# Sums of the second pass's right-hand blocks: made beside the output layer and kept in DRAM, or made beside the first down layer

## The chip, the cores and the metric

The kernel runs on one core of one Trainium2 chip. The metric is the time of one execution in microseconds, as the device measures it. All products run on TensorE in single precision (fp32r operands, fp32 sums in PSUM).

## The reference

`q`, `k`, `v` have 4 batches, 12 heads, 448 positions and 64 channels; the token matrix `x` has 1792 rows (4 batches of 448) and 768 columns.

```python
attn = sigmoid(q @ k.T / 8 - log(448)) @ v          # per batch and head, then heads side by side: x
xn   = x / sqrt(mean(x*x) + 1e-6) * rms_g
g    = xn @ w_gate                                  # 768 -> 1536
y    = (g * sigmoid(g) * (xn @ w_val)) @ w_out      # 1536 -> 768
a, b = y @ w1, y @ w2                               # 768 -> 1024
out  = (a * b @ w3) @ moe2_w_out                    # 1024 -> 1024 -> 768
```

The kernel multiplies `w3` by the second `w_out` once and keeps the product in DRAM, so that the last two layers are one layer of 1024 to 768.

## The kernel before, in words

**Tiles.** Activations lie transposed: 128 channels by the 448 tokens of one batch (0.22 MB in fp32). Each operand of an exact product is a pair of fp32r tiles, a high part (a copy on ScalarE) and a low part (the block less its high part: on VectorE for activations, on GpSimd for most weights), and each product of two 128-wide blocks is three matmuls of 448 columns: high by high, low by high, high by low (`runs`, L340, whose matmul is L346).

**Passes.** Batches 0 and 1 are the first pass (g = 0), batches 2 and 3 the second (g = 1). Where a layer is worked by Strassen-Winograd, the two batches of the pass are the two columns of blocks, and seven products stand for eight. The output layer of the first block is not: its second pass, `b_units(1)`, is twelve groups of 36 matmuls (`b_group`, L810), `j` 0 to 11, with m = j // 2 the block of 128 output channels and b = j % 2 the batch. A group's result goes from PSUM to a scratch tile on ScalarE (`yf`, L815) and by a DMA of SyncE's queue to DRAM (`yd`, L817).

**The layers after it**, in program order: eight `c_winograd` for the first pass (`a` and `b` of `y`, the up layers), three `d_winograd(0)` (the first down layer, which writes the first half of the output), eight `c_winograd` for the second pass and three `d_winograd(1)`. In the up layers a product is 9 matmuls (L689 calls `runs`), in the down layers 6; each Winograd step has seven products, and a `d_winograd` runs them twice, the second time adding to the same seven PSUM banks. `combine` (L716) takes the seven results from PSUM: one by ScalarE (`u`, L722) and the rest by VectorE (`v` L725, `c` L729, `u` L732, `c` L735, `u` L739, `v` L740 and L744). A bank is free for the next product when the instruction that reads it is done.

**Right-hand blocks.** An up layer needs for each k of 0 to 2 seven right-hand tiles, from the four blocks of `y` that belong to k (m = k and k + 3, both batches): the four blocks themselves and four sums of them. Each of the seven becomes a high part (ScalarE, L584) and a low part (VectorE, L576): 21 such pairs. For the first pass this is `y_blocks(0, k)` (L655), which runs beside the output layer of the second pass, after j = 2, 5 and 8. For the second pass it is `y_steps(k)` (L668), spread over the first down layer by `step` (L661): `combine` and `d_winograd` call `step` once per product, and each call runs the first generator of the list `todo` up to its next `yield`. Before that list reaches `y_steps`, it ends `right_steps` for the down layer's own operands.

**Buffers and order.** `held` (L92) is a tag of four buffers of one block each; the blocks of `y` come through it, and so do three of every four products `a * b` in the up layers (`ab`, L764). `scratch` (L89) is a tag of six. The Tile framework decides each engine's order by a planner, which takes instructions as its model sees them ready, in the order of the program where several are; an instruction may thus come long before its place in the program. `tc.keep_in_program_order` ties an instruction behind the one traced before it on its engine; the subtractions of `y_steps` are tied so. Each engine, and SyncE's queue with nearly all DMAs, then works its list strictly in order.

Of the kernel before, what the change touches and what calls it, by code (L numbers as in the profile page):

```python
# [9 lines left out]
F32 = mybir.dt.float32  # L10
F32R = mybir.dt.float32r
U32 = mybir.dt.uint32
AF = mybir.ActivationFunctionType
ALU = mybir.AluOpType
PSUM = bass.MemoryType.PSUM

B, H, S, D = 4, 12, 448, 64
P = 128
# [27 lines left out]
def fused_kernel(ctx: ExitStack, tc: tile.TileContext, qkv, wg, wv, wo, w1, w2, w3, wo2, gam, out):  # L46
    nc = tc.nc
# [15 lines left out]
    dram = tc.alloc_tile_pool(name="dram", bufs=1, space=bass.MemoryType.DRAM)  # L63
# [21 lines left out]
    def parts(pool, tag, bufs, name, w=S, step=0):  # L85

        return pool.tile([P, 2, w + step], F32R, tag=tag, bufs=bufs, name=name)[:, :, :w]

    def scratch(name):  # L89
        return scr.tile([P, S], F32, tag="s", bufs=6, name=name)  # L90

    def held(name):  # L92
        return scr.tile([P, S], F32, tag="held", bufs=4, name=name)
# [438 lines left out]
    acts = {}  # L532

    def x_tile(name, b):
        return parts(r1a, "x0", 6, name, step=STEP) if b == 0 else parts(r1b, "x1", 6, name)
# [24 lines left out]
    def right_tile(name, bl):  # L560
        p, n, step = {0: (r1a, 6, STEP), 1: (r1b, 6, 0), 2: (pools["xw"], 9, STEP)}[bl]
        return parts(p, f"x{bl}", n, name, step=step)

    def ab_tile(name, n):

        if n < 2 * KF1:
            return h_tile(name, n // 2)
        return right_tile(name, (n - 2 * KF1) // 2)

    def right_steps(k, b, home=None, down=False, wait=None):  # L570

        def sub(out, in0, in1, op=ALU.subtract):
            i = nc.vector.tensor_tensor(out=out, in0=in0, in1=in1, op=op)  # L576
            if down or wait is not None:
                tc.keep_in_program_order(i)

        late = []  # L580

        def put(j, bl, src):
            t = acts["d" if down else "w", j, k] = ab_tile(f"w{j}", 7 * k + j) if down else right_tile(f"w{j}", bl)
            nc.scalar.activation(t[:, 0, :], src, AF.Copy)  # L584
            low()
            late.append((t, src))

        def low():
            if late:
                t, src = late.pop()  # L590
                sub(t[:, 1, :], src, t[:, 0, :])

        if wait is None:
            put(0, 0, b[0])
            yield
            t1 = home()
            sub(t1, b[1], b[0])
            put(5, 1, t1)
            yield
            while len(b) < 4:  # L600
                low()
                yield
            put(2, 0, b[2])
            yield
            t3 = home()
            sub(t3, b[3], b[1])
            put(3, 2, t3)
            yield
            t2 = home()
            sub(t2, t3, b[0], ALU.add)  # L610
            put(1, 2, t2)
            yield
            t4 = home()
            sub(t4, b[2], t2)
            put(4, 2, t4)
            yield
            put(6, 1, b[3])
            yield
            low()
            return  # L620
        t1 = scratch("t1")
        sub(t1, b[1], b[0])
        t2 = scratch("t2")
        sub(t2, b[3], t1)
        put(1, 2, t2)
        yield
        sub(b[1], b[3], b[1])
        put(3, 2, b[1])
        yield
        sub(t2, b[2], t2)  # L630
        put(4, 2, t2)
        yield
        for _ in range(wait):
            low()
            yield
        for j, bl, x in ((0, 0, b[0]), (2, 0, b[2]), (5, 1, t1), (6, 1, b[3])):
            put(j, bl, x)
            yield
        low()

    def x_blocks(k):
        for _ in right_steps(k, [load_x(b, m) for m in (k, k + 3) for b in (2, 3)], bank):
            pass

    yd = {}

    def load_y(g, k):
        y = []
        for m in (k, k + 3):
            for b in range(2):  # L650
                y.append(held("ys"))
                nc.sync.dma_start(out=y[-1], in_=yd.pop((g, b, m)))
        return y

    def y_blocks(g, k):  # L655
        for _ in right_steps(k, load_y(g, k), bank):
            pass
# [3 lines left out]
    def step():  # L661

        if todo:
            next(todo[0], None)
            if inspect.getgeneratorstate(todo[0]) == inspect.GEN_CLOSED:
                todo.pop(0)

    def y_steps(k):  # L668
        y = load_y(1, k)
        for _ in range(2):  # L670
            yield
        yield from right_steps(k, y, wait=5 if k == 2 else 0)

    def product_bank():
        return psm()[:, :S]
# [149 lines left out]
    def b_units(g):  # L825
        for m in range(KD):
            for b in range(2):
                yield 6.8, (lambda m=m, b=b: b_group(g, m, b)), (i_b2 if g else i_b)[m][1]

    def run(unit, more=0):  # L830
        cost, fn, wi = unit
        W.load_to(wi + 2 + more)
        fn()
        W.split_to(wi + 1 + more)
        W.load_to(wi + 3 + more)
        return cost
# [50 lines left out]
    for k in range(KD):  # L887
        t = acts["x", 1, k] = x_tile("x", 1)
# [24 lines left out]
    b = list(b_units(0))  # L913
# [35 lines left out]
    for j, u in enumerate(b_units(1)):  # L949
        run(u, 1)  # L950
        if j in (2, 5, 8):
            y_blocks(0, j // 3)


    for m in range(KF2):
        c_winograd(i_c, m)
    todo.extend(y_steps(k) for k in range(KD // 2))
    for n in range(KD // 2):
        d_winograd(0, i_d, n)
# [64 lines left out]
```

## Time and profile before

| | |
|---|---|
| median of 3 runs | 1059.55 us (1058.46 to 1061.62) |
| the profiled execution | 1058.72 us, of which the span from the first to the last instruction is 1056.9 us |
| busy, share of the span | PE 99%, PEld 84%, DVE 77%, ACT 42%, POOL 38% |
| output layer, second pass | 654.1 to 742.3 us |
| up layers, first pass | 742.3 to 845.1 us |
| first down layer | 845.1 to 899.1 us |

How to read it: PE is TensorE's matmul row and PEld its weight loads, DVE is VectorE, ACT ScalarE, POOL GpSimd and SP SyncE, which issues the DMAs. PE's busy time includes modelled ends of pipelined matmuls, so it can hide small waits; the number of matmuls in a stretch, or the busy time of PEld, shows them. A wait is listed with the engine that waits and, behind the arrow, what released it.

### The profile page before, as it was taken

The numbers are of one execution on the slowest core, as the hardware profiler recorded it, in microseconds if no ns is written. First come the engines' busy times: TensorE is split into PE (matmuls) and PEld (weight loads), VectorE is DVE, ScalarE is ACT, GpSimd is POOL, SyncE is SP. The second block draws the span as 40 slices with busy tenths as digits, with TensorE's granted clock in tenths as the row PEclk, the third lists the DMA queues.
The fourth block names the chain that finished last, engine by engine and source line by source line (L and its number), as shares of the span: only waits on it lengthen the run. The fifth ranks groups of instructions, "written<-read, shape, count | busy, mean of one in ns | idle before, by whom it ended". The sixth has DMA issues, their size and how long they took to land. (4 is left out here: it accounts for less than half of the span.)

```text
span 1056.9 us, 14300 instructions
## 1 busy us (share of the span) xinstructions
PE 1047.1 (99%) x5150; PEld 890.0 (84%) x5150; DVE 813.6 (77%) x1172; ACT 442.2 (42%) x800; POOL 398.9 (38%) x342
## 2 busy tenths in 40 slices
PE   9999999999999999999999999999999999999998
PEld 4338799998777777798999999999999998999997
DVE  5998988777665787788677778973688999677764
ACT  5684332223454553335444443332344455344431
POOL 2646400000222221102555554232555666555562
PEclk9999999999999999999999999999999999999999
DMA  7653555665454567763122113867333344533131
GB/s 262 243 185 106 180 185 182 209 225 206 146 164 147 182 216 253 251 231 111 65 65 71 69 68 105 273 230 245 129 120 120 94 132 144 164 108 115 52 95 70
DMA packets 72934, 164.26 MB, mean 155 GB/s; under 512 B 7200, under 2 KB 45216, under 8 KB 72864
## 3 DMA queue, kind: packets, MB, share of 16 engines
q1 hardware_dynamic: 70560, 160.20, 45.6%
q10 hardware_dynamic: 2304, 3.15, 0.8%
q8 instruction: 41, 0.67, 0.3%
q14 instruction: 29, 0.24, 0.1%
HBM read 119.67 MB, written 43.65 MB: 155 GB/s over the span
## 5 line engine op out<-in xcount | busy, mean ns | idle before, releaser
L346 PE MATMUL w<-w,ws 128*128 128x448 f32 x2052 | 420.6, 366 | 1.6 <-DVE v L725 1.6
L346 PEld LDWEIGHTS w<-w,ws 128*128 128x128 f32 x2052 | 385.0, 188 | 35.1 <-DVE v L725 2.0
L139 POOL TENSOR_TENSOR ws<-wd,ws 128x384 fp32r<-128x384 f32 (+1 forms) x160 | 154.7, 983 | 157.0 <-ACT ws L135 146.3
L346 PE MATMUL psm<-hm,ws 128*128 128x448 f32 x864 | 178.3, 367 | 0.5 <-DVE ws L139 0.5
L346 PEld LDWEIGHTS psm<-hm,ws 128*128 128x128 f32 x864 | 161.9, 188 | 16.7 <-issue 2.0
L346 PE MATMUL psm<-x,ws 128*128 128x448 f32 x648 | 136.3, 368 | 0.4 <-DVE s L794 0.4
L346 PEld LDWEIGHTS psm<-x,ws 128*128 128x128 f32 x648 | 120.9, 188 | 15.1 <-issue 2.9
L139 POOL TENSOR_TENSOR ws<-wf,ws 128x768 fp32r<-128x768 f32 (+1 forms) x51 | 94.7, 1860 | 98.5 <-ACT ws L135 97.5
L135 ACT ACTIVATE ws<-wf 128x768 fp32r<-128x768 f32 (+1 forms) x81 | 66.5, 825 | 99.5 <-PE psm L346 21.1
L135 ACT ACTIVATE ws<-wd 128x384 fp32r<-128x384 f32 (+1 forms) x160 | 71.0, 476 | 65.7 <-PE w L346 47.0
L428 POOL TENSOR_TENSOR qk<-qk 128x960 fp32r<-128x960 f32 x10 | 23.8, 2381 | 189.9 <-ACT qk L427 189.9
L115 DVE TENSOR_SCALAR mag<-wd 128x768 uint32<-128x768 uint32 (+1 forms) x76 | 47.1, 619 | 49.1 <-DMA wd<-in_wo 18.1
L139 POOL TENSOR_TENSOR ws<-s,ws 128x384 fp32r<-128x384 f32 (+1 forms) x64 | 63.4, 990 | 49.3 <-ACT ws L135 45.9
L125 DVE SCALAR_TENSOR_TENSOR wf<-wd,wf 128x768 uint32<-128x768 uint32 (+1 forms) x76 | 79.4, 1045 | 2.3
L117 DVE TENSOR_SCALAR wf<-mag 128x768 uint32<-128x768 uint32 (+1 forms) x76 | 62.6, 823 | 16.3 <-POOL ws L139 11.1
L128 DVE SCALAR_TENSOR_TENSOR wf<-wd,wf 128x768 uint32<-128x768 uint32 (+1 forms) x76 | 73.6, 969 | 1.1
L346 PEld LDWEIGHTS psm<-o,ws 128*128 128x128 f32 x384 | 67.3, 188 | 2.4 <-issue 2.3
L346 PE MATMUL psm<-o,ws 128*128 128x384 f32 x384 | 69.3, 339 | 0.0
L509 POOL TENSOR_TENSOR acc<-acc,sq 128x448 f32<-128x448 f32 x20 | 27.1, 1357 | 85.0 <-ACT sq L508 85.0
L180 DVE TENSOR_TENSOR wd<-wd,s 128x384 f32<-128x384 f32 (+1 forms) x32 | 26.8, 837 | 33.8 <-POOL ws L139 33.8
L116 DVE TENSOR_SCALAR mag<-mag 128x768 f32<-128x768 f32 (+1 forms) x76 | 50.6, 665 | 1.7
L462 ACT ACTIVATE a<-sc,bias_s 128x896 f32<-128x896 f32 x48 | 45.4, 997 | 8.4 <-PE sc L442 8.4
(122 smaller groups left out, 1278.1 us busy)
## 6 DMA issues: line engine op xcount, KB each, us to landing
wd<-in_wo SPq DMA_DIRECT2D x20, 768.0 KB, 5.4
wd<-in_w SPq DMA_DIRECT2D x16, 768.0 KB, 5.3
wd<-in_wg SPq DMA_DIRECT2D x12, 768.0 KB, 4.5
wd<-in_wv SPq DMA_DIRECT2D x12, 768.0 KB, 5.2
raw<-in_qkv SPq DMA_DIRECT2D x12, 736.0 KB, 4.3
wd<-in_w SPq DMA_DIRECT2D x16, 512.0 KB, 4.4
w<-wf SPq DMA_DIRECT2D x16, 384.0 KB, 2.6
wd<-w SPq DMA_DIRECT2D x16, 384.0 KB, 3.5
```

The costliest lines, as they stand in the source:

```text
L115: nc.vector.tensor_scalar(out=mag.bitcast(U32), in0=hi, scalar1=0x7FFFFFFF, scalar2=None, op0=ALU.bitwise_and)
L116: nc.vector.tensor_scalar(out=mag, in0=mag, scalar1=HI_MIN, scalar2=HI_MAX, op0=ALU.max, op1=ALU.min)
L117: nc.vector.tensor_scalar(out=u, in0=mag.bitcast(U32), scalar1=3, scalar2=0x3FFFFFFF, op0=ALU.logical_shift_left, op1=ALU.bitwise_and,)
L125: nc.vector.scalar_tensor_tensor(out=u, in0=hi, scalar=0xC0000000, in1=u, op0=ALU.bitwise_and, op1=ALU.bitwise_or)
L128: nc.vector.scalar_tensor_tensor(out=u, in0=lo, scalar=29, in1=u, op0=ALU.logical_shift_right, op1=ALU.bitwise_or)
L135: nc.scalar.activation(t[:, 0, :w], f[:, :w], AF.Copy)
L139: lows.tensor_tensor(out=t[:, 1, :w], in0=f[:, :w], in1=t[:, 0, :w], op=ALU.subtract)
L180: nc.vector.tensor_tensor(out=a12, in0=a12, in1=s2, op=ALU.subtract)
L346: nc.tensor.matmul(ps, w, xt[:, xi, :], start=first and r == 0 and j == 0, stop=last and r == 2 and j == n - 1)
L428: nc.gpsimd.tensor_tensor(out=lo, in0=x, in1=hi, op=ALU.subtract)
L462: nc.scalar.activation(a, both, **sigmoid)
L509: nc.gpsimd.tensor_tensor(out=acc[b], in0=acc[b], in1=sq, op=ALU.add)
```

## The change

`right_steps` loses its second form, in which the seven tiles came in another order with the sums made in place; it now serves the first pass and the down layers alone. A new function `y_sums(k)` loads the four blocks of the second pass for k, makes the four sums on VectorE and stores them in DRAM. It is called in the output layer after the groups j = 7 (k = 0) and j = 9 (k = 1), and after the last group (k = 2). `y_steps(k)` then loads seven blocks (three sums first, then the four others, the last sum among these) one by one, three ahead, and only copies and subtracts.

```diff
-    def right_steps(k, b, home=None, down=False, wait=None):
+    def right_steps(k, b, home, down=False):
...
-        t1 = scratch("t1")
-        sub(t1, b[1], b[0])
-        t2 = scratch("t2")
-        sub(t2, b[3], t1)
-        put(1, 2, t2)
-        yield
-        sub(b[1], b[3], b[1])
-        put(3, 2, b[1])
-        yield
-        sub(t2, b[2], t2)
-        put(4, 2, t2)
-        yield
-        for _ in range(wait):
-            low()
-            yield
-        for j, bl, x in ((0, 0, b[0]), (2, 0, b[2]), (5, 1, t1), (6, 1, b[3])):
-            put(j, bl, x)
-            yield
...
+    y_src = {}
+
+    def y_sums(k):
+
+        src = y_src[k] = {j: yd[1, b, m] for j, (b, m) in zip((0, 5, 2, 6), ((0, k), (1, k), (0, k + 3), (1, k + 3)))}
+        y = load_y(1, k)
+        t1, t2, t4 = (scratch(n) for n in ("t1", "t2", "t4"))
+        tt = nc.vector.tensor_tensor
+        tt(out=t1, in0=y[1], in1=y[0], op=ALU.subtract)
+        tt(out=t2, in0=y[3], in1=t1, op=ALU.subtract)
+        tt(out=y[1], in0=y[3], in1=y[1], op=ALU.subtract)
+        tt(out=t4, in0=y[2], in1=t2, op=ALU.subtract)
+        for j, t in ((1, t2), (3, y[1]), (4, t4), (5, t1)):
+            src[j] = dram.tile([P, S], F32, name=f"ysum{k}{j}")
+            nc.sync.dma_start(out=src[j], in_=t)
+
     def y_steps(k):
-        y = load_y(1, k)
+
+        late, order = [], ((1, 2), (3, 2), (4, 2), (0, 0), (2, 0), (5, 1), (6, 1))
+
+        def load(n):
+            t = held("ys")
+            nc.sync.dma_start(out=t, in_=y_src[k][order[n][0]])
+            return t
+
+        def low():
+            if late:
+                t, src = late.pop()
+                tc.keep_in_program_order(nc.vector.tensor_tensor(out=t[:, 1, :], in0=src, in1=t[:, 0, :], op=ALU.subtract))
+
+        blocks = [load(n) for n in range(3)]
         for _ in range(2):
             yield
-        yield from right_steps(k, y, wait=5 if k == 2 else 0)
+        for n, (j, bl) in enumerate(order):
+            for _ in range(5 if n == 3 and k == 2 else 0):
+                low()
+                yield
+            t = acts["w", j, k] = right_tile(f"w{j}", bl)
+            src = blocks.pop(0)
+            nc.scalar.activation(t[:, 0, :], src, AF.Copy)
+            low()
+            late.append((t, src))
+            if n + 3 < len(order):
+                blocks.append(load(n + 3))
+            yield
+        low()
...
         if j in (2, 5, 8):
             y_blocks(0, j // 3)
+        if j in (7, 9):
+            y_sums((j - 7) // 2)
+    y_sums(2)
```

## Rows read from the trace of the kernel before

**Rows 1.** The page's first part: busy us (share of the span) xinstructions.
```profile
PE 1047.1 (99%) x5150; PEld 890.0 (84%) x5150; DVE 813.6 (77%) x1172; ACT 442.2 (42%) x800; POOL 398.9 (38%) x342
```

**Rows 2.** Who waited for whom, PE alone, 654 to 900 us.
```profile
PE w L346 <- DVE v L725: 1.6, 1, 1.6
PE psm L346 <- DVE c L735: 0.2, 1, 0.2
```

**Rows 3.** Busy time by stretch: length, then PE, PEld, DVE, ACT, POOL; clock, DMA.
```profile
654.00:742.30 88.30, 88.30 (x435) 81.22 (x434) 62.11 (x89) 26.66 (x48) 27.07 (x16) 1.00 0.70 240
742.30:845.10 102.80, 102.80 (x505) 94.50 (x504) 85.80 (x136) 41.64 (x90) 59.62 (x59) 1.00 0.37 118
845.10:899.10 54.00, 52.19 (x254) 46.91 (x253) 51.60 (x80) 27.55 (x65) 35.66 (x36) 1.00 0.47 141
...
879.47:890.53 11.06, 9.25 (x43) 7.57 (x42) 10.59 (x20) 2.14 (x7) 7.18 (x8) 1.00 0.67 209
```

**Rows 4.** The chain that ended last: start, duration, engine, tile, line, instructions.
```profile
899.24 107.59 PE w L346 x528
```

**Rows 5.** PE in order of time in the first down layer: start, duration.
```profile
870.92 5.04 PE L346 MATMUL w<-w,ws 128*128 128x448 f32 x24
...
879.47 1.40 PE L346 MATMUL w<-w,ws 128*128 128x448 f32 x6
882.44 3.98 PE L346 MATMUL w<-w,ws 128*128 128x448 f32 x18 [1.57 <-DVE v L725]
```

**Rows 6.** VectorE in order of time, the same stretch.
```profile
871.03 1.16 DVE L576 TENSOR_TENSOR t<-ys 128x448 f32<-128x448 f32 x1
...
881.77 0.61 DVE L725 TENSOR_TENSOR v<-w,u 128x448 f32<-128x448 f32 x1
```

**Rows 7.** VectorE by shape, 845 to 899 us: busy us, mean ns, idle before.
```profile
L576 DVE TENSOR_TENSOR t<-ys,t 128x448 f32<-128x448 f32 x6 | 4.2, 701 | 0.5 <-DMA ys<-y 0.4
...
L576 DVE TENSOR_TENSOR ys<-ys 128x448 f32<-128x448 f32 x3 | 2.4, 798 | 0.0
L576 DVE TENSOR_TENSOR t<-ys 128x448 f32<-128x448 f32 x3 | 2.4, 797 | 0.0
```

**Rows 8.** Tile ys, 845 to 899 us: its queue instruction, issue to landing.
```profile
L652 SPq DMA_DIRECT2D ys<-y x11: 319/332/455, 850.1 to 886.1; - x11
DMA to landing us min/median/max: 2.4/2.9/4.6
```

**Rows 9.** Tile yf, 654 to 760 us: its store, issue to landing.
```profile
DMA to landing us min/median/max: 1.9/3.4/5.2
```

**Rows 10.** Who waited for whom, SyncE's queue, 844 to 899 us.
```profile
SPq L652 <- DVE t L576: 7.6, 3, 6.1
```

**Rows 11.** ScalarE in order of time, output layer.
```profile
713.08 0.53 ACT L815 ACTIVATE yf<-psm 128x448 f32<-128x448 f32 x1
719.65 0.85 ACT L135 ACTIVATE ws<-wf 128x768 fp32r<-128x768 f32 x1 [6.04 <-DMA wf<-wo]
```

**Rows 12.** SyncE's queue in order of time, output layer.
```profile
715.22 0.86 SPq L817 DMA_DIRECT2D y<-yf  x2
```

**Rows 13.** VectorE in order of time: y_blocks(0, 2), first and last of its eleven.
```profile
698.94 0.63 DVE L576 TENSOR_TENSOR w<-ys 128x448 f32<-128x448 f32 x1 [0.49 <-DMA ys<-y]
...
703.45 1.33 DVE L576 TENSOR_TENSOR w<-w,w 128x448 fp32r<-128x448 f32 x2
```

**Rows 14.** All engines in order of time around the start of the up layers.
```profile
742.46 0.54 ACT L815 ACTIVATE yf<-psm 128x448 f32<-128x448 f32 x1 [2.63 <-PE psm L346]
...
743.59 0.40 SPq L817 DMA_DIRECT2D y<-yf  x1
...
746.19 0.62 DVE L725 TENSOR_TENSOR v<-w,u 128x448 f32<-128x448 f32 x1 [3.06 <-PE w L346]
...
757.04 0.63 DVE L744 TENSOR_TENSOR psm<-w,v 128x448 f32<-128x448 f32 x1
758.04 0.62 DVE L764 TENSOR_TENSOR ab<-psm,u 128x448 f32<-128x448 f32 x1
```

More of the change, by code (lines that the diff above doesn't have):

```diff
@@ L568, in ab_tile @@
         return right_tile(name, (n - 2 * KF1) // 2)
-    def right_steps(k, b, home=None, down=False, wait=None):
+    def right_steps(k, b, home, down=False):
         def sub(out, in0, in1, op=ALU.subtract):
             i = nc.vector.tensor_tensor(out=out, in0=in0, in1=in1, op=op)
-            if down or wait is not None:
+            if down:
                 tc.keep_in_program_order(i)
@@ L591, in low @@
                 sub(t[:, 1, :], src, t[:, 0, :])
-        if wait is None:
-            put(0, 0, b[0])
-            yield
-            t1 = home()
-            sub(t1, b[1], b[0])
-            put(5, 1, t1)
-            yield
-            while len(b) < 4:
-                low()
-                yield
-            put(2, 0, b[2])
-            yield
-            t3 = home()
-            sub(t3, b[3], b[1])
-            put(3, 2, t3)
-            yield
-            t2 = home()
-            sub(t2, t3, b[0], ALU.add)
-            put(1, 2, t2)
-            yield
[L613 to L620, printed above, removed]
-        t1 = scratch("t1")
-        sub(t1, b[1], b[0])
-        t2 = scratch("t2")
-        sub(t2, b[3], t1)
+        put(0, 0, b[0])
+        yield
+        t1 = home()
+        sub(t1, b[1], b[0])
+        put(5, 1, t1)
+        yield
+        while len(b) < 4:
+            low()
+            yield
+        put(2, 0, b[2])
+        yield
+        t3 = home()
+        sub(t3, b[3], b[1])
+        put(3, 2, t3)
+        yield
+        t2 = home()
+        sub(t2, t3, b[0], ALU.add)
         put(1, 2, t2)
         yield
-        sub(b[1], b[3], b[1])
-        put(3, 2, b[1])
+        t4 = home()
+        sub(t4, b[2], t2)
+        put(4, 2, t4)
         yield
-        sub(t2, b[2], t2)
-        put(4, 2, t2)
+        put(6, 1, b[3])
         yield
-        for _ in range(wait):
-            low()
-            yield
-        for j, bl, x in ((0, 0, b[0]), (2, 0, b[2]), (5, 1, t1), (6, 1, b[3])):
-            put(j, bl, x)
-            yield
         low()
@@ L666, in step @@
                 todo.pop(0)
-    def y_steps(k):
-        y = load_y(1, k)
+    y_src = {}
[11 more added lines that the diff above has]
+            nc.sync.dma_start(out=src[j], in_=t)
+    def y_steps(k):
+        late, order = [], ((1, 2), (3, 2), (4, 2), (0, 0), (2, 0), (5, 1), (6, 1))
[8 more added lines that the diff above has]
+        blocks = [load(n) for n in range(3)]
         for _ in range(2):
             yield
-        yield from right_steps(k, y, wait=5 if k == 2 else 0)
+        for n, (j, bl) in enumerate(order):
+            for _ in range(5 if n == 3 and k == 2 else 0):
+                low()
+                yield
+            t = acts["w", j, k] = right_tile(f"w{j}", bl)
[5 more added lines that the diff above has]
+                blocks.append(load(n + 3))
+            yield
+        low()
     def product_bank():
```

## The prediction

> **What bounds the kernel now.** I read the page's first part, then the waits of PE, then the stretches, and last the order of time around the one stretch that stood out. PE is busy for 99% of the span [rows 1], so only time that PE loses can be won. From the output layer to the end of the first down layer PE's own waits are two, 1.6 us for VectorE's `v` (L725) and 0.2 us for `c` (L735), both in the first down layer [rows 2].
>
> The stretches show the same loss in another way. The undisturbed rate of matmuls is on the chain of waits: 528 in 107.59 us, 0.2038 us each [rows 4]. The first down layer is 3 steps x 2 x 7 products x 6 matmuls = 252 matmuls, which is 51.35 us at that rate; the stretch takes 54.00 [rows 3]. It loses 2.65 us, 2.50 of them in one window of 42 matmuls, which should be 8.56 us and is 11.06 [rows 3]. VectorE is busy there for 51.60 of 54.00 us (96%), against 70% in the output layer (62.11 of 88.30) and 83% in the up layers [rows 3]. So in the first down layer VectorE is the limit, and nowhere near the change does PE lose anything else.
>
> Here two readings differ. PE's busy time says 1.81 us is lost (54.00 less 52.19) [rows 3]; the weight loads say more: 94.50 of 102.80 us (91.9%) in the up layers, so 49.64 would be due in 54.00, and 46.91 are there, 2.73 us missing [rows 3]. The Trainium skill, Perfetto Trace Analysis, section Identifying the Most-Contended Engine, says that a matmul row's busy share is no good measure of headroom and the weight loads' share is. By its rule the most to be won is 2.7 us, by PE's busy time 1.8; the count of matmuls above agrees with the rule.
>
> **How the stall comes about.** In the fourth run of seven products (from 870.92 us) the second product ends at 870.92 + 12 x 0.204 = 873.4 us [rows 5]. VectorE takes it from its bank only at 881.77 [rows 6], 8.4 us later. The next step's second product wants that bank at 879.47 + 1.22 = 880.7 and starts at 882.44 [rows 5]: 1.75 us late. Ahead of `v` on VectorE stand the tied subtractions of `y_steps`, the sums for k = 1 from 871.03 on among them [rows 6].
>
> **What the change removes there.** Four sums for each k, twelve in all: 4.2 + 2.4 + 2.4 = 9.0 us, 0.75 each [rows 7]. VectorE's load falls to 42.6 of 54 us, 79%, below the 83% at which the up layers run without a wait of PE. Eight of the twelve (k = 0 and 1) stand before the late `v`: 6.0 us less ahead of it, where 1.75 would do. The wait goes, with 4.25 us to spare. Gain: 2.5 us, up to 2.65; the sum takes 2.4, as some of the small losses around it may not be VectorE's.
>
> **What it adds there.** 21 loads for 12, so nine more of 0.22 MB, 2 MB in 54 us on DMA engines at 47% [rows 3]: about 38 GB/s on 141. ScalarE's copies and the low parts are as many as before. New is that each low part hangs on its own load. The loads n = 4 to 6 of each k wait until the low part of block n - 4 is done, which is traced with the copy of block n - 3, three products (3.66 us) before the copy that wants the load. A load takes 0.33 us of issue and 2.9 us to land (2.4 to 4.6) [rows 8]: 3.23 us, inside by 0.4 at the median, late by 1.27 at the longest. The first load of a next k is traced two products (2.44 us) before its copy: late by 0.8 at the median and 2.5 at the longest, if the planner doesn't bring it forward; the two behind it have a product more each. A late load holds ScalarE's copy, and behind it the weights' high parts; then the tied low part, and behind it on VectorE `v`, `c` and `u`, which free PE's banks. Ahead of the `v` in question are three loads of the first kind (k = 0) and one of the second (k = 1). From both sides: nothing, or 3 x 1.27 + 2.5 = 6.3 us, more than the 4.25 spare. At the medians it is 0.8, which the spare covers, so I take nothing.
>
> SyncE's queue is in order, and the loads stand in it among the stores of the output and the loads of weights. Before the change a load of `ys` held that queue for up to 6.1 us while a buffer was in use [rows 10]. Now each load wants one buffer where four were wanted together; I cost this at nothing, and at one such hold, 6.1 us less the spare 4.25, about 1.9, on the other side.
>
> **What it adds in the output layer.** Twelve sums (7 to 9 us) on a VectorE with 26 us idle of 88; twelve loads and twelve stores on DMA engines at 70% [rows 3]. PE needs neither. Weights are far ahead: the high part split at 719.65 is for matmuls some 12 us later (the last of twelve halves, first used half way into the group j = 10; groups are 88.2 / 12 = 7.35 us, so at 742.3 - 11.0 = 731.3) [rows 11], so SyncE's queue may be held some microseconds. Cost nothing.
>
> The loads read what was just stored. For j = 7 ScalarE's copy is at 713.08 [rows 11] and its store issued at 715.22 [rows 12]; landing takes 3.4 us (1.9 to 5.2) [rows 9], and then the load its 3.2. So `y_sums(0)` has its last block at about 722. It comes before `y_blocks(0, 2)` in the program, and both want all four `held` buffers. If the planner gives them in that order, `y_blocks(0, 2)`, now at 698.94 to 704.8 on VectorE [rows 13], moves behind it: three sums to 724.5, a store to 728 (it frees y[1]), a load to 731.5, then 6 us of work as now: 737.5. The first up layer starts at 742.3 [rows 14]: 4.8 us to spare. Cost nothing.
>
> `y_sums(2)` falls into the first up layer: result copied at 742.46, stored from 743.59 [rows 14], landed 747, loaded 750.2, sums of 2.5 us on VectorE by 753. VectorE takes a product there 0.3 us after it is done (`v` at 746.19 for a product done at 742.26 + 3.67) [rows 14], and a bank is wanted again three products, 5.5 us, later. So 2.5 us of sums fit, and a blocked VectorE costs PE only beyond about 3 to 4.5 us: the seventh product, done at 755.1 and read until 757.67 [rows 14], is wanted back at about 760.5, 2.9 us on. Cost nothing; on the other side 3 us, if the last load is late by a landing more.
>
> **The sum.** Profiled execution 1058.72 us (span 1056.9 and 1.8 around it) less 2.4 is 1056.3. That execution is 0.8 us under the median of the runs, so on the median, 1059.55, I forecast 1057.1.
>
> **Rivals.**
> Loads take the place of the sums. If the new loads ahead of that `v` are late by more than the 4.25 us spare together (of 6.3 at the longest), the stall at 880.7 comes back for another reason. For: the median has only 0.4 us in hand, and a hold of SyncE's queue adds to it. Against: the planner may issue a load as soon as its buffer is free, and products without a copy between two k's let it catch up. Time: 1059.5, 1061 with one hold of the queue.
>
> The buffers' chain, the slower one. `held` goes from `y_sums(0)` to `y_blocks(0, 2)`, `y_sums(1)`, `y_sums(2)` and the first `ab` (second one at 758.04 [rows 14]), each time over a store and a load. It decides at 742.3 us: two holds of SyncE's queue of the longest kind shown, 6.1 us [rows 10], are 12.2 us against the 4.8 to spare, so PE would wait 7.4 us for the first up layer's operands. With the 2.4 won later: 1059.55 + 7.4 - 2.4 = 1064.5. For: five users of four buffers in 45 us, each behind a DMA. Against: VectorE and SyncE have much idle time there, and the planner knows of the buffers. The Trainium skill, DMA: Bandwidth & Descriptors, section Anatomy of one DMA — SWDGE (gpsimd) path, speaks for this rival: a DMA signals only once its last byte is confirmed in the target, slowest where that is HBM, so a block stored and read back pays that twice. By its fit (2.0 us and bytes over 436 GB/s) an estimate is 2.5 us a landing, 5 for both; the rows have 3.4 and 2.9 [rows 8, 9], so the trace is dearer still.
>
> The sums do not leave the busy stretch: the planner puts them late, with the stall unchanged: 1059.5. Against: in the output layer all their inputs but those of k = 2 are there over 100 us before use.
>
> **How the numbers follow.** Forecast 0.63; late loads 0.16; the buffers' chain 0.17; sums that stay 0.04. A measurement of this kernel tells about 0.3% from no change, 3.2 us. The most that can be won, 2.65, is under that; with the runs' spread of 3 us a quarter of the forecast's cases still measures as faster: 0.15. Slower by over 3.2 us is the buffers' chain from 5.6 us of waiting on, 0.12, and late loads that hold more than these bounds, 0.04: 0.16. Within: 0.69. The range: 1055.4 (2.65 won, and 1.5 for the spread of the runs) to 1062.0, which takes in late loads with one hold and leaves out most of the slow chain.
>
> **What would show it.** Right: no wait of PE for L725 in the first down layer; the stretch at 51.4 to 51.7 us for its 252 matmuls; VectorE near 79% there with idle time behind loads of `ys`; the output layer at 88 and the up layers at 102.8 us. Wrong: a PE gap at the start of the first up layer, or a low part waiting on `ys` ahead of a late `v`.

## The result, and the profile after

The changed kernel takes 1070.46 us (median of 5 runs, 1069.48 to 1073.44), the kernel before beside it 1059.82 (5 runs, 1058.46 to 1061.62): ratio 1.0106, 95% interval 1.0090 to 1.0121. The forecast was 1057.1 with a range to 1062.0. It is slower, by about 10.6 us, and the sign was wrong.

The profiled execution after took 1072.52 us, its span is 1070.6. Against the span before, 1056.9, the 13.7 us divide so, by four marks: the first matmul of the output layer, the first of the up layers, the first into a `psm` tile of the first down layer, and the last of that layer:

| stretch | before | after | difference |
|---|---|---|---|
| start to output layer | 654.08 | 656.13 | +2.05 |
| output layer | 88.18 | 88.18 | 0 |
| start of the up layers to the down layer's `psm` | 107.74 | 120.48 | +12.74 |
| first down layer | 49.08 | 47.91 | -1.17 |
| the rest | 157.8 | 157.9 | +0.1 |

The 2.05 us ahead of the output layer lie where the program is the same. Of the kernels below, some that are no slower start their up layers as late, at 744.97 and 743.80 against 742.26, so I take this as a spread between executions and not as the change's. The question is the 12.74.

The first view is the page's first part; it answers to [rows 1]: busy us, share of the span, instructions.
```profile
PE 1050.7 (98%) x5150; PEld 891.7 (83%) x5150; DVE 812.5 (76%) x1172; ACT 442.5 (41%) x800; POOL 393.0 (37%) x342
```
The counts are those of before: the change only moves instructions. VectorE is as busy as ever, so this line names no culprit. PE's waits from 656 to 930 us do, as in [rows 2]: engine and line, who released it, us in total, times, the longest.
```profile
PE w L346 <- DVE v L744: 6.7, 1, 6.7
PE w L346 <- ACT u L741: 2.4, 1, 2.4
PE w L346 <- DVE u L751: 0.6, 1, 0.6
PE psm L346 <- DVE c L754: 0.3, 1, 0.3
```
`v` (L744) is the `v` of L725 before, `u` (L741) that of L722. The name is the one that the forecast expected to vanish, but the place is another: in order of time PE shows both waits just after the start of the up layers, after 36 and 45 matmuls (four and five products) (start, duration; in brackets the idle time before, and its releaser).
```profile
744.31 7.50 PE L346 MATMUL w<-w,ws 128*128 128x448 f32 x36
754.20 3.14 PE L346 MATMUL w<-w,ws 128*128 128x448 f32 x9 [2.40 <-ACT u L741]
764.07 36.13 PE L346 MATMUL w<-w,ws 128*128 128x448 f32 x166 [6.72 <-DVE v L744]
```
The waits are 9.1 us of the 12.74. The rest stands in the stretches (length, then busy us and instructions of PE, PEld, DVE, ACT and POOL, granted clock, DMA share, GB/s), which answer to [rows 3]:
```profile
764.07:769.68 5.61, 5.61 (x18) 5.04 (x18) 3.65 (x7) 1.51 (x3) 1.19 (x2) 0.60 0.38 124
...
864.79:912.70 47.91, 47.10 (x230) 42.59 (x228) 38.37 (x62) 26.12 (x60) 29.86 (x33) 1.00 0.66 198
```
After the waits TensorE runs at a granted clock of 0.60: 18 matmuls in 5.61 us, where 18 x 0.2038 = 3.67 are due [rows 4], 1.9 lost. The nine of 754.20 took 3.14 us for 1.83, 1.3 lost. 9.1 + 1.9 + 1.3 = 12.3 of 12.74. The last line is the first down layer: PEld 42.59 of 47.91 us (88.9%) against 86.9% before [rows 3], whose stretch begins 24 matmuls earlier, and VectorE is 80% busy.

Who holds `v`? VectorE in order of time, from just before the wait to its end:
```profile
753.06 0.61 DVE L654 TENSOR_TENSOR t<-ys 128x448 f32<-128x448 f32 x1
755.53 1.34 DVE L180 TENSOR_TENSOR wd<-wd,s 128x384 f32<-128x384 f32 x1 [1.86 <-POOL ws L139]
761.78 0.63 DVE L655 TENSOR_TENSOR t<-ys,t 128x448 f32<-128x448 f32 x1 [4.90 <-DMA ys<-y]
...
763.39 0.62 DVE L744 TENSOR_TENSOR v<-w,u 128x448 f32<-128x448 f32 x1
```
L654 to L657 are the sums of `y_sums(2)`. They stand ahead of `v` in VectorE's list, and the second of them waits for the last block of `y`, which reached SBUF at 761.8. SyncE's queue in order of time shows why so late:
```profile
749.16 0.32 SPq L660 DMA_DIRECT2D ysum<-t  x1
749.60 0.37 SPq L836 DMA_DIRECT2D y<-yf  x1
...
753.17 0.40 SPq L177 DMA_DIRECT2D sums<-wd  x1
...
754.49 0.69 SPq L836 DMA_DIRECT2D y<-yf  x1
...
759.33 0.32 SPq L630 DMA_DIRECT2D ys<-y  x1
```
The last block is stored at 754.49 and asked for again at 759.33. ScalarE had its copy ready at 747.12 + 0.53 = 747.65, by its own order of time:
```profile
747.12 0.53 ACT L834 ACTIVATE yf<-psm 128x448 f32<-128x448 f32 x1
...
752.79 0.52 ACT L135 ACTIVATE ws<-s 128x384 fp32r<-128x384 f32 x1 [4.31 <-DVE s L173]
...
753.63 0.52 ACT L741 ACTIVATE u<-w 128x448 f32<-128x448 f32 x1
```
So the store is 6.8 us late, and in the queue it comes behind `sums<-wd` (L177), whose operand VectorE made only after the sums of `y_sums(1)`; the store before it, of block j = 10, stands right behind the last store of a sum of k = 1 (749.16). Before, the store of the last block followed its copy in 0.6 us [rows 14]. The last two rows are those of PE's shorter wait: `u` stands on ScalarE behind the high part of a weight, which waited 4.31 us for VectorE's `s` (L173), and VectorE worked that after the same sums of `y_sums(1)`.

### The profile page after: what moved, and what is told of

It is laid out like the page before. It is cut to its first block, busy times and chain, and to the rows that moved or that the text cites. A ratio compares the mean times of both kernels' runs of the same rounds, so it can differ in the third digit from the quotient of the medians.

```text
span 1070.6 us, 14355 instructions
## 1 busy us (share of the span) xinstructions
PE 1050.7 (98%) x5150; PEld 891.7 (83%) x5150; DVE 812.5 (76%) x1172; ACT 442.5 (41%) x800; POOL 393.0 (37%) x342
## 5 line engine op out<-in xcount | busy, mean ns | idle before, releaser
L115 DVE TENSOR_SCALAR mag<-wd 128x768 uint32<-128x768 uint32 (+1 forms) x76 | 44.9, 591 | 51.9 <-DMA wd<-in_wo 19.5
L117 DVE TENSOR_SCALAR wf<-mag 128x768 uint32<-128x768 uint32 (+1 forms) x76 | 59.8, 786 | 24.3 <-POOL ws L139 19.0
L116 DVE TENSOR_SCALAR mag<-mag 128x768 f32<-128x768 f32 (+1 forms) x76 | 53.6, 705 | 1.7
```

What stands on the lines that cost most here:

```text
L115: nc.vector.tensor_scalar(out=mag.bitcast(U32), in0=hi, scalar1=0x7FFFFFFF, scalar2=None, op0=ALU.bitwise_and)
L116: nc.vector.tensor_scalar(out=mag, in0=mag, scalar1=HI_MIN, scalar2=HI_MAX, op0=ALU.max, op1=ALU.min)
L117: nc.vector.tensor_scalar(out=u, in0=mag.bitcast(U32), scalar1=3, scalar2=0x3FFFFFFF, op0=ALU.logical_shift_left, op1=ALU.bitwise_and,)
```

## The experiments

Five theories, by the letters that the records below use. All take it that `v` is late because the sums of k = 2 are ahead of it. A: the last block's way to DRAM and back alone makes them late. B: the four `held` buffers, with `y_blocks(0, 2)` moved behind `y_sums(0)`, make ScalarE's copies late. C: SyncE's queue has more DMAs than it can issue in time. D: the stores of the last blocks of `y` stand in the queue behind stores of sums, which wait for VectorE. E: any other sums in the output layer suffice to make those of k = 2 late. Ratios are to the kernel before, with 95% intervals.

| run | edit | us | ratio | PE's waits at the start of the up layers |
|---|---|---|---|---|
| the change | | 1070.46 | 1.0106 (1.0090 to 1.0121) | 2.4 + 6.7 |
| e1_k2_back | k = 2 as before | 1059.88 | 1.0000 (0.9987 to 1.0014) | 1.4 |
| e2_only_k2 | k = 0, 1 as before | 1060.60 | 1.0008 (0.9998 to 1.0017) | none |
| e3_last_block_kept | last block stays in SBUF | 1068.46 | 1.0087 (1.0069 to 1.0105) | 3.5 + 7.2 |
| e4_k2_later | sums of k = 2 behind the second up step | 1061.58 | 1.0016 (1.0005 to 1.0026) | 1.0 |
| e5_blocks_first | `y_sums(0)` behind `y_blocks(0, 2)` | 1070.70 | 1.0106 (1.0090 to 1.0123) | 8.7 |
| e6_blocks_first_k01 | e5 and e1 | 1057.06 | 0.9977 (0.9968 to 0.9986) | none |
| e7_own_buffers_k2 | own buffers for k = 2 | 1070.11 | 1.0099 (1.0080 to 1.0118) | 1.8 + 6.7 |
| e8_stores_other_queue | stores of `y` from ScalarE's queue | 1074.35 | 1.0146 (1.0127 to 1.0165) | 7.2 + 5.3 |
| e9_blocks_first_k02 | e5, with k = 1 as before | 1064.47 | 1.0043 (1.0028 to 1.0058) | 3.2 |
| e10_k1_stores_last | e5, stores of k = 1's sums behind those of `y` | 1065.86 | 1.0061 (1.0040 to 1.0083) | 6.1 + 1.1 |
| e11_blocks_first_k2_later | e5 and e4 | 1057.62 | 0.9991 (0.9982 to 1.0001) | none |
| e12_two_loads_ahead | e6, loads two ahead, not three | 1056.47 | 0.9972 (0.9962 to 0.9983) | none |

**Which k, and where.** e1 gives k = 2 its old form back (loads, sums and copies in the first down layer) and keeps `y_sums` for k = 0 and 1; e2 is the other way round. e4 keeps all twelve sums out of the down layer, but ties those of k = 2 behind the second up step, in buffers of another tag.
```diff
# e1 (e2: SUMS = (2,))
+    SUMS = (0, 1)
     def y_steps(k):
+        return (y_steps_new if k in SUMS else y_steps_old)(k)
...
-        if j in (7, 9):
+        if j in (7, 9) and (j - 7) // 2 in SUMS:
             y_sums((j - 7) // 2)
-    y_sums(2)
+    if 2 in SUMS:
+        y_sums(2)
# e4: h=True takes buffers of tag "h" and ties the sums
-    y_sums(2)
...
+        if m == 1:
+            y_sums(2, True)
```


> The changed kernel, but the sums for k = 2 are made in the first down layer again, as before the change; those for k = 0 and 1 stay beside the output layer. Theory A (the sums for k = 2 stand on VectorE ahead of the first v of the up layers and wait for a block that is just being stored and loaded back): PE has no wait over 1 us at the start of the up layers, the granted clock stays 1.0 there, and the time is 1057.5 to 1060, as the first down layer keeps a part of its 1.2 us. Theory B (the four held buffers: y_sums(0) and y_sums(1) push y_blocks(0, 2) and the stores of y late, so the start of the up layers is late whatever k = 2 does): a wait of PE of 3 to 9 us stays there, time 1063 to 1070.

> The other half: only the sums for k = 2 are made after the output layer, those for k = 0 and 1 in the first down layer as before. Theory A: PE still waits for the first v of the up layers, less than 9.1 us since the last store of y no longer stands behind the chain of k = 1 in SyncE's queue: copied 744.5, stored 745, landed 749, loaded back 752.5, three sums, v at 754.3 where 751.4 is wanted: 2 to 4 us of waiting, some loss by a lower clock behind it, 1061 to 1066. Theory B: no wait there, 1058 to 1060.

> The changed kernel, but the sums for k = 2 are tied behind the second step of the up layers on VectorE, and their four blocks lie in two buffers that the output layer's operands have left, so they hold none of the four held buffers. Theory A: no wait of PE over 1 us at the start of the up layers, and the first down layer keeps its gain of 1.2 us or more: 1057 to 1060. Theory B: y_sums(0) and y_sums(1) still come ahead of y_blocks(0, 2): a wait of 3 us or more stays, 1063 to 1069.

Measured: each of the three takes 9 to 11 us off the change. Of the forecasts only A's time for e1 came in, by a hair (its wait, 1.4 us, did not); the waits that A had for e2 and B for e1 and e4 are not there, e2's time is 0.6 us above B's range and e4's 1.6 above A's. e2 is the telling one: with `y_sums(2)` just where the change has it, PE doesn't wait. SyncE's queue of e2 in order of time, the store of the last block and its load:
```profile
745.16 0.38 SPq L869 DMA_DIRECT2D y<-yf  x1
...
747.27 0.32 SPq L652 DMA_DIRECT2D ys<-y  x1
```
VectorE of e2, the sum that needs this block, and `v` (L777 there):
```profile
750.82 0.62 DVE L677 TENSOR_TENSOR t<-ys,t 128x448 f32<-128x448 f32 x1
...
752.42 0.62 DVE L777 TENSOR_TENSOR v<-w,u 128x448 f32<-128x448 f32 x1
```
The copy ended at 744.55, the store follows at 745.16, and `v` comes at 752.42, 11 us earlier than in the changed kernel. So `y_sums(2)` ahead of `v` costs nothing by itself; it costs when the sums of k = 0 and 1 are there too. And these alone (e1) give no such wait: both are needed. Two smaller losses: in e1 the first down layer takes 46.55 us, 2.5 less than before, and the up layers 2.4 more (1.4 us of wait for VectorE's `psm` after six products among them), which is why its sum is nought; and e4's up layers take 109.90 us, 2.2 more, with `y_sums(0)` ahead of `y_blocks(0, 2)` as in e1.

**The block's way back, and the buffers.** e3 keeps the last block, j = 11, in its buffer for `y_sums(2)`, without store and load. e7 gives the four blocks of k = 2 buffers that nothing else uses then. e5 puts `y_sums(0)` behind `y_blocks(0, 2)`, and `y_sums(1)` stays.
```diff
# e3
-        y = scratch("yf")
+        y = kept_y[g, b, m] = (held if g and m == KD - 1 and b else scratch)("yf")
...
+                if (g, b, m) == (1, 1, KD - 1):
+                    y.append(kept_y[g, b, m])
+                    continue
# e7
-        y = load_y(1, k)
+        y = load_h(k) if h else load_y(1, k)
...
-    y_sums(2)
+    y_sums(2, True)
# e5
-        if j in (7, 9):
-            y_sums((j - 7) // 2)
+        if j in (8, 9):
+            y_sums(j - 8)
```


> The changed kernel, but the last block of y (j = 11) is kept in its tile on the chip for the sums of k = 2 instead of being read back from DRAM (it is stored as well, for the later load). VectorE's order stays: the three sums before v. Theory A: the wait for the load goes, what remains is the sums themselves (2 us on VectorE) and the late copy: at most 3 us of PE's 9.1 stay, and the clock's loss goes with them: 1058 to 1062. Theory B: 1067 to 1071, as the copy, the buffers and the queue are as they were.

> The changed kernel, but the four blocks for the sums of k = 2 lie in two buffers that the output layer's operands have left, not in the four held ones; order of calls and DMAs as in the changed kernel. Theory B: y_blocks(0, 2) still waits behind y_sums(0), the copies and stores of j = 10 and 11 stay late, and PE waits 5 to 9 us: 1064 to 1070. If instead the hand-over of the held buffers from y_sums(1) to y_sums(2) is what is late: under 3 us of wait, 1058 to 1062.

> The changed kernel with one call moved: y_sums(0) comes behind y_blocks(0, 2) in the program (both after j = 8), so that y_blocks(0, 2) gets the four held buffers first; the sums for k = 1 and 2 and every DMA stay. Theory B, as the four runs before leave it (y_blocks(0, 2) waits behind y_sums(0) for the held buffers, ScalarE's copies of y for j = 9 to 11 stand behind it in order, so their stores and all of y_sums(2) come late): y_blocks(0, 2) is on VectorE at 699 to 706 us again, the copies of j = 10 and 11 follow their groups within 1 us, PE waits under 2 us at the start of the up layers, 1057 to 1060. Theory C (twelve more loads and twelve more stores are too much for SyncE's queue in order, wherever they come from): the last store of y stays 5 us or more behind its copy, PE waits 5 us or more, 1065 to 1070.

Measured: all three stay within 2 us of the change. e3's time and e7's waits (8.5 us together) are what B had forecast; it is e5 that decides against B. In e3 the loads of the other blocks stood behind the late store (at 755.40) and the first sum began at 761.01 in place of the second at 761.78; theory A falls. With buffers of its own (e7) k = 2 waits as long: to take it out of the four buffers is not enough. In e5 the last seven of the eleven instructions of `y_blocks(0, 2)` are back at 704 to 710 us and ScalarE's last two copies are prompt, yet `v` is as late. B falls too, for this wait. With those two copies prompt, e5 shows the chain best. ScalarE, the copies of j = 9, 10 and 11, and a weight's high part ahead of the first:
```profile
735.71 0.53 ACT L135 ACTIVATE ws<-s 128x384 fp32r<-128x384 f32 x1 [4.52 <-DVE s L173]
736.14 0.53 ACT L834 ACTIVATE yf<-psm 128x448 f32<-128x448 f32 x1
...
738.50 0.55 ACT L834 ACTIVATE yf<-psm 128x448 f32<-128x448 f32 x1 [1.00 <-PE psm L346]
...
745.82 0.54 ACT L834 ACTIVATE yf<-psm 128x448 f32<-128x448 f32 x1 [2.63 <-PE psm L346]
```
SyncE's queue of e5 (L836 stores a block of `y`, L630 loads blocks, L660 stores a sum):
```profile
738.81 0.58 SPq L836 DMA_DIRECT2D y<-yf  x1
...
742.69 1.54 SPq L630 DMA_DIRECT2D ys<-y  x2
...
749.75 0.32 SPq L660 DMA_DIRECT2D ysum<-t  x1
750.16 0.38 SPq L836 DMA_DIRECT2D y<-yf  x1
...
...
754.30 0.49 SPq L836 DMA_DIRECT2D y<-yf  x1
...
758.68 0.32 SPq L630 DMA_DIRECT2D ys<-y  x1
```
VectorE of e5, the second sums of k = 1 and of k = 2, and `v`:
```profile
746.39 0.63 DVE L655 TENSOR_TENSOR t<-ys,t 128x448 f32<-128x448 f32 x1 [5.86 <-DMA ys<-y]
...
761.32 0.63 DVE L655 TENSOR_TENSOR t<-ys,t 128x448 f32<-128x448 f32 x1 [6.04 <-issue]
...
762.93 0.62 DVE L744 TENSOR_TENSOR v<-w,u 128x448 f32<-128x448 f32 x1
```
Read across the three: the store of block j = 9 (738.81), its load for k = 1 once that has landed (742.69), the sum of it when the load has landed (746.39), the stores of these sums (to 749.75), and only behind them in the queue the store of block j = 10, which ScalarE had ready at 739.05: 11.1 us late. Block j = 11, ready at 746.36, is stored at 754.30, behind stores of weight sums (L177) that VectorE made after the same sums. Then its landing, its load (758.68), and the sums of k = 2 at 761.32. One store-load-sum chain stands in an in-order queue ahead of the start of the next one.

The first chain starts late itself. The up layers begin at 745.62 in e5, so the group j = 9 ends two groups before, 72 x 0.2038 = 14.7 us, at 730.9; its copy comes 5.2 us later, behind a high part that waited for VectorE's `s`, and VectorE worked that `s` right after the sums of k = 0. With k = 0's sums in that place (the change, e5, e6, e9, e10) this copy is 4.0 to 8.8 us late; before the change and in e2, 0.6.

The Trainium skill, Perfetto Trace Analysis, section DMA Instruction — HWDGE (DVE, Sync), says that a DMA's semaphore wait is on the issuing sequencer, which is free for its next instruction only after that DMA's issue. The trace agrees: nothing of the queue passes the stores that wait for VectorE, and a finished block lies 11.1 us behind them.

**The queue's order.** If D is right, moving the stores of `y` out of the way should help. e8 issues those of the second pass from ScalarE's queue; e10 (on e5) issues the four stores of k = 1's sums behind the last store of `y`.
```diff
# e8
-        nc.sync.dma_start(out=d, in_=y)
+        (nc.scalar if g else nc.sync).dma_start(out=d, in_=y)
# e10
+    with tc.issue_after(last_y[0]):
+        stores()
```


> The changed kernel, but the stores of y of the second pass are issued from ScalarE's DMA queue right behind their copies, so they stand behind nothing on SyncE's queue. Theory B: the copies of j = 10 and 11 are as late as in the changed kernel (2 to 9 us behind their groups), so PE still waits 3 to 7 us: 1062 to 1068. Theory C: the store follows its copy at once, the last block is back 6 to 7 us earlier and PE's wait goes to under 2 us: 1058 to 1061.

> All three k, y_blocks(0, 2) first, and the four stores of the sums for k = 1 are queued on SyncE's queue behind the last store of y; sums, loads and VectorE's order ahead of v stay. Theory D: the stores of j = 10 and 11 follow their copies within 2 us, PE's wait goes from 8.7 us to under 3, the clock's loss goes with most of it: 1057 to 1063. Theory E: 7 to 9 us as before, 1068 to 1071.

Measured: e8 is slower still, and e10 is 4.8 us faster than e5 by the medians. Both forecasts for e8 miss; for e10 D's miss, and E's is right in the waits (7.2 us) and 2 us too high in the time. Neither run took a wait away without setting another. ScalarE in order of time in e8 (ACTq is its queue's issue):
```profile
747.88 0.53 ACT L834 ACTIVATE yf<-psm 128x448 f32<-128x448 f32 x1
...
755.29 0.35 ACTq L836 DMA_DIRECT2D y<-yf  x1
755.69 0.52 ACT L135 ACTIVATE ws<-wd 128x384 fp32r<-128x384 f32 x1 [6.88 <-DMA wf<-sums]
```
The store of j = 11 is issued 6.9 us after its copy on this queue too, and everything of ScalarE's behind it, `u` included, waits with it: PE's first wait, for `u`, is now 7.2 us. What held it is not in the rows by name; the trace puts ScalarE's idle time down to a landing of another DMA. In e10 ScalarE's `u` waits for a scratch buffer that k = 1's sums, not yet stored, still occupy (ScalarE in order of time):
```profile
757.84 0.54 ACT L748 ACTIVATE u<-w 128x448 f32<-128x448 f32 x1 [4.88 <-DMA ysum<-t]
```
PE waits 6.1 us for it, and for `v` 1.1 in place of 8.7. But `v` itself is no earlier than in e5, 17.6 us after the first matmul of the up layers (744.86) against 17.3: PE only comes to it later. VectorE of e10:
```profile
762.41 0.62 DVE L751 TENSOR_TENSOR v<-w,u 128x448 f32<-128x448 f32 x1
```
And the stores of `y` are as late, though no store of a sum of k = 1 is ahead of them. SyncE's queue of e10 (L845 stores a block of `y`, L630 loads one), and the queue's longest wait from 745 to 750 us:
```profile
748.98 0.32 SPq L630 DMA_DIRECT2D ys<-y  x1
749.39 0.38 SPq L845 DMA_DIRECT2D y<-yf  x1
```
```profile
SPq L630 <- DVE ys L656: 2.6, 1, 2.6
```
Block j = 10, copied by 738.27, is again stored 11.1 us late (749.39), and j = 11, copied by 745.60, 8.7 us late (754.28). A load of k = 2 now stands ahead of them, which waits for a `held` buffer until a sum of k = 1 (L656) is done. So D, as worded, is not the cause: without its stores the queue is held by the next instruction that hangs on the sums of k = 1, and these are as late as in e5 (the second at 746.40 against 746.39). What e8 and e10 can't show is a queue in which nothing hangs on them.

**How many sums make it late.** e9 has `y_sums` for k = 0 and 2 in e5's places, so no store of k = 1's sums is ahead of `y`'s.
```diff
-    SUMS = (0, 1)
+    SUMS = (0, 2)
...
+        if j == 8:
+            y_sums(0)
```


> y_blocks(0, 2) first as in the run with that name, but now the sums for k = 0 and 2 are made ahead and those for k = 1 in the first down layer, as before the change. Theory D (what the runs leave: the stores of y for j = 10 and 11 stand in SyncE's queue behind the stores of the sums for k = 1, these behind VectorE, and VectorE behind the block of j = 9, which is being stored and loaded back; so the block of j = 11 is back 14 us after its copy, and the sums of k = 2 hold v): without k = 1 the stores of j = 10 and 11 are issued within 1.5 us of their copies, PE waits under 0.5 us at the start of the up layers, 1057 to 1060. Theory E (the sums for k = 2 ahead of v, with any other sums and their DMAs ahead of them, are enough): 5 us of waiting or more, 1064 to 1070.

Measured: between the two. The wait for `v` is 3.2 us; with the granted clock at 0.98 over the up layers, these take 5.0 us more than before (112.77). D said under 0.5 us and E at least 5, so both miss: with k = 0's sums alone beside those of k = 2 a third of the loss is there (the late copy of j = 9 above is one way), with k = 1's all of it. C is weakened too, without having had a run of its own: e11 below issues all of the change's DMAs and has no wait.

**The two cures.** e6 is e1 in e5's order: sums for k = 0 and 1 only, `y_sums(0)` behind `y_blocks(0, 2)`. e11 has all twelve sums, k = 2's behind the second up step. e12 is e6 with the loads in the down layer two ahead, for the rival that late loads cost there.
```diff
# e6: SUMS = (0, 1), and
+        if j in (8, 9):
+            y_sums(j - 8)
# e11: the same lines, and behind the second up step
+        if m == 1:
+            y_sums(2, True)
# e12, on e6
-        blocks = [load(n) for n in range(3)]
+        blocks = [load(n) for n in range(2)]
...
-            if n + 3 < len(order):
-                blocks.append(load(n + 3))
+            if n + 2 < len(order):
+                blocks.append(load(n + 2))
```


> As the run above, but the sums for k = 2 are made in the first down layer again, as before the change. With k = 2 back in the first down layer and y_sums(0) ahead, that layer lost nothing (46.5 us for 228 matmuls, 2.7 less than before) and the up layers lost 2.4. Theory B: that loss came from y_blocks(0, 2) being late and goes: up layers 107.7 us, first down layer 46.5, time 1056.5 to 1058, the fastest of all. Theory C: with two thirds of the DMAs the loss in the up layers stays at 2 us or more, 1059 to 1060.

> All twelve sums out of the first down layer: k = 0 and 1 behind y_blocks(0, 2), k = 2 tied behind the second step of the up layers, in two buffers that the output layer's operands have left. Theory D: no sums of k = 2 ahead of the first v, so no wait over 0.5 us at the start of the up layers (up layers 107.7 to 108.3 us); the first down layer at 47 to 48 us for 228 matmuls as in the changed kernel: 1057 to 1059. Theory E: the same here.

> The fastest run so far (y_blocks(0, 2) first, k = 0 and 1 ahead, 1057.1), with the loads in the first down layer two ahead instead of three. If the loads land just in time with three, as the prediction had it (3.23 of 3.66 us), two products (2.44 us) are 0.8 us too few for each of ten loads: first down layer 48 to 52 us instead of 46.7, 1058.5 to 1062. If the planner brings the loads forward, or VectorE's spare takes the lateness up, it stays at 46.7 to 47.2 and the time at 1057.

Measured: no wait at the start of the up layers in any of the three. The stretches of e6, the up layers and the first down layer (columns as above):
```profile
743.16:850.92 107.76, 107.76 (x529) 99.04 (x528) 93.51 (x148) 43.94 (x96) 62.64 (x62) 1.00 0.40 128
850.92:897.59 46.67, 46.67 (x230) 42.65 (x229) 41.31 (x65) 25.42 (x59) 30.93 (x33) 1.00 0.63 188
```
The same two of e11:
```profile
744.97:852.71 107.74, 107.74 (x530) 99.04 (x528) 95.47 (x152) 43.94 (x96) 64.04 (x62) 1.00 0.46 147
852.71:900.92 48.21, 47.10 (x229) 42.59 (x228) 39.22 (x63) 26.09 (x60) 30.49 (x33) 1.00 0.66 197
```
The up layers are back at 107.74 to 107.76 us, what they took before to 0.02 us, and e1's 2.4 us went with the order of two calls, as B's forecast for e6 had it (1057.06 in 1056.5 to 1058). e11's time is as forecast too; e12 refutes late loads there (48 to 52 us forecast). In e6 the stores of j = 10 and 11 are still late (744.78 and 747.84, for copies done at 736.59 and 743.91), but nothing of VectorE's waits for them. That settles the place: the loss needs the sums of k = 2 ahead of `v`, and sums of k = 0 and 1 that delay the last blocks of `y`. e6 and e12 are faster than the kernel before, by 0.23% (0.14 to 0.32) and 0.28% (0.17 to 0.38); the two can't be told apart, so a third load ahead shows no worth here.

## Why the prediction was wrong

**The stall in the first down layer: right.** PE's wait of 1.6 us for `v` is gone from that layer in the change, and in e6 and e12, where no wait of PE is left from 656 to 930 us, it takes 46.67 and 46.55 us against 49.08: 2.4 and 2.5 won, the forecast's term 2.4. That e6's median, 1057.06, is the forecast's 1057.1 is no hit: it is another version than the one forecast. In the change itself only 1.17 was won: with k = 2 on the new loads too PE waits 0.6 us for `u` and 0.3 for `c` (e11: 0.9 and 0.2), which the forecast did not have.

**VectorE at 79%: right** (38.37 of 47.91, 80%).

**The loads in the down layer at nothing: right for k = 0 and 1.** e6 and e12 have no wait there. The rival of late loads is refuted for them; for k = 2 a late load does cost something, in the way that the prediction described for its first rival. After the change, ScalarE, then VectorE, ahead of PE's wait at 898:
```profile
894.08 1.76 ACT L685 ACTIVATE w<-ys 128x448 fp32r<-128x448 f32 x3 [2.24 <-DMA ys<-ysum]
...
897.00 0.95 DVE L172 TENSOR_TENSOR s<-wd 128x256 f32<-128x256 f32 x1 [1.68 <-POOL ws L139]
897.87 0.61 DVE L751 TENSOR_TENSOR u<-w,v 128x448 f32<-128x448 f32 x1
```
The copy waits for a sum of k = 2 from DRAM, the weights' high parts come behind it, GpSimd's low part waits 3.0 us for them, VectorE's `s` for that, and `u` behind `s`: 0.6 us of PE. e11 shows the same row by row, with 0.9.

**The output layer at nothing: right as far as it went.** It takes 88.18 us as before, and the first up layer starts without a wait, though `y_blocks(0, 2)` ended at 743.3 in place of the forecast 737.5. (Its "6 us of work as now" was a misreading: 698.94, which [rows 13] has as the first of its eleven, is the fifth, the first is at 689.33. In the change the eleven take from 730.5 to 743.3.) The step counted what the output layer loses, but not what the sums leave behind in SyncE's queue.

**`y_sums(2)` at nothing: this is the step that failed.** It took the last block "stored from 743.59", as before the change [rows 14], and the sums done by 753; the bound on the other side was 3 us. e2 shows that reckoning right on its own premise: there the sums are done at 752.5. In the change, where the up layers start 2.05 us later, the store is issued at 754.49 and the sums end at 763.5. The forecast put the sums of k = 0 and 1 and those of k = 2 in separate terms, each at nothing, and did not follow the queue that joins them: store, load and sum of k = 1, what waits for these sums in the queue (their stores, or a load for a buffer that they still read), then the stores of the last two blocks, then the load of k = 2. Its bound let the last load be late "by a landing more"; it was late by a whole second chain.

**What the wait costs: too small.** Past a free time of about 3 us a wait was priced at its own length. The granted clock added 3.2 us to 9.1.

**The rivals.** The slower one named the right place and nearly the right price (7.4 us of wait against 9.1), but not the mechanism: it decided by the `held` buffers, which e7 clears and e5 clears another way, both without effect (in e10 they hold the queue, but in the place of something else), and by operands of the up layer, while PE waited for banks that `v` should have freed. Its chance, 0.17, was too low, as it was priced as two exceptional holds of the queue; here five loads that wait for a landing hold it 9.6 us from 715 to 765 us. The Trainium skill, DMA: Bandwidth & Descriptors, section Anatomy of one DMA — SWDGE (gpsimd) path, has the fit that stands beside this rival for DMAs of GpSimd's path, and these are SyncE's. The prediction went by its rows; in the change the last block takes 4.8 us from its store's issue to its load's, and 2.5 from there to the sum.

**What stays open.** Which of the holds ahead of the late stores weighs most was not separated: the lateness of VectorE's sums of k = 1 and what hangs on them, the loads that wait for a landing, or other landings, as e8's second queue suggests. e10 shows only that one hold steps into the place of another. Each edit of one link (e3, e5, e7, e8, e10) left PE waits of 7 us or more together.

## What to carry to other kernels

Work that is stored and loaded back through one in-order queue joins edits that look separate: walk that queue instruction by instruction, with what each one waits for, from the moved work to the next use of the engine it feeds. Ask of each moved instruction not only whether its engine has time, but what stands behind it in the engine's list when its last operand is late: here three late sums held back the one instruction that frees PE's banks. And test a many-part change by parts and by pairs of parts: e1 and e2 each lost nothing, and together they lose 1%.

## What the hardware showed besides

TensorE's granted clock fell to its lower level, 0.50 (1.2 of 2.4 GHz), around two waits of 2.4 and 6.7 us. Stretches of two us (columns as above, the granted clock third from the end):
```profile
754.00:756.00 2.00, 1.80 (x6) 1.65 (x7) 0.47 (x1) 0.98 (x3) 2.00 (x3) 0.73 0.87 311
756.00:758.00 2.00, 1.35 (x4) 0.66 (x2) 0.87 (x1) 0.00 (x0) 1.73 (x2) 0.50 1.07 392
...
766.00:768.00 2.00, 2.00 (x7) 1.74 (x7) 0.79 (x2) 0.69 (x2) 0.00 (x0) 0.50 0.12 45
768.00:770.00 2.00, 2.00 (x10) 1.84 (x9) 1.45 (x3) 0.83 (x2) 1.51 (x2) 0.86 0.00 0
770.00:772.00 2.00, 2.00 (x12) 1.83 (x11) 1.97 (x4) 0.08 (x1) 0.47 (x1) 1.00 0.24 46
```
It fell within 1.8 us of PE's return from the first, shorter wait (754.20), and after the second it was back 4 to 6 us after PE's return (764.07). In the kernel before, waits of 1.6 and 0.2 us left the clock at 1.00 [rows 2, 3].
